# Linear attention beside a long convolution: denominators by groups of 512 tokens, new homes for the weights, and a new order of units

## The chip, the cores and the metric

The kernel runs on one core of a Trainium2 chip. The time is that of one execution on the device, in microseconds. A profiled execution gives a trace beside it: the span from its first to its last instruction, every instruction on every engine, and every DMA packet. The engines are PE (matrix products; its weight loads are listed as PEld), DVE, ACT and POOL (elementwise work), and SP, whose queue issues all DMAs of this kernel.

## What is computed

Two independent blocks, side by side in the output. Sequence length 2048, width 576, everything in bf16.

```python
# A: shift filter of 4 taps on k, times v, long causal convolution with ssm_k, times q
k_shift = sum(k_pad[:, t:t + S, :] * shift_k[:, 3 - t] for t in range(4))
kv = k_shift * v
y = irfft(rfft(kv, 2 * S) * rfft(ssm_k, 2 * S))[:S] + kv * ssm_D
a = q * y
# B: linear attention, 32 heads of 18
q, k, v = split(x @ wqkv)
phi = lambda t: where(t > 0, t + 1, exp(t)) + 1e-6
kv = einsum("bhsd,bhde", phi(k), v);  z = phi(k).sum(s)
o = (phi(q) @ kv) / ((phi(q) . z) + 1e-6)
b = o @ wo
return concatenate([a, b], -1)
```

## The kernel before, in words

The program is a list of units, `ORDER`. A unit is a name with arguments and, behind `@`, the PSUM banks (eight of 2 KB a partition) that its tiles take. The units are written out in that order, and each engine and the SP queue run their own instructions in the order of the list. An engine that must wait holds up everything behind it on that engine and nothing else. All waits follow from the data: an input must have been written, and a bank or a buffer must have been read to the end before it is written again.

**Block A.** The convolution is done with transforms as matrix products, in five chunks of channels (`ACH`: 128, 128, 64, 128, 128; chunk number is the first argument).

- `hl` loads ssm_k of a chunk and its D column. `hT` (L477) adds D to the first tap on ACT, turns the chunk with 16 PE transposes and evicts it.
- `h1`, `u1` (`s1`, L489): eight matmuls of 128 columns with the table G, for the filter h and the signal u = kv; the eviction goes to a tile C.
- `ht`, `ut` (`tr`, L503): SP issues a DMA transpose of half of C into a tile Ct. There are two Ct buffers, shared by h and u. The tag `c8` has two buffers as well, shared by C of h, C of u and V (L280), so a C can only be written when the transposes of an older one have landed.
- `h2`, `u2` (`s2`, L511): eight matmuls of 512 columns with 64x32 weights out of Ct into T or SU. `pX`, `pT` (`prod`, L526): products on DVE or POOL. `i1` and `j1` (L537, L551): 64 matmuls each of 64 columns, in four row groups; `j1` also evicts into V.
- `i2` (L562): 16 or 32 matmuls back to time, multiplied on DVE into q in place. `st` stores.
- `cv` (`conv`, L454): the four taps, in stages 0 to 3, eight operations of 128x2048 a chunk, each on DVE (`D`) or POOL (`P`). `Wj` (L376) spreads the taps over 128 partitions with matmuls whose weight is a row of ones. `kl`, `vl`, `ql` load k, v, q in two groups of channels; q takes the buffer of v.
- `io`, `ix`, `sin`, `iw`, `iv`, `wk`, `sw`, `W`, `FT`, `id` make the tables: index work on DVE and POOL, sines on ACT. `iv` (L186) has eight small operations on POOL (L192, L195) and one on DVE; `sw` (L217) takes the last sine and then loads the table of the exponential, so no exponential can come before it.

**Block B.** x is needed as it is (`xl`, L314, tile `x_sb`) and turned (`xT`, two buffers of 512 tokens). The turned x comes from `xd` (`x_D`, L342), two DMA transposes from DRAM and a memset on POOL for each group of 512 tokens. The functions `x_T` and `x_T2` (L325, L334) that turn it on PE stand in the file, but no unit calls them.

- `q` and `k` (L446, L430): five matmuls of 512 columns each; `kt` (L437) makes the last 64 columns of k for four token tiles. `phi` (L425) is an exponential on ACT and a min/max on DVE.
- `Gt` and `G` (L613, L627): x transposed times phi(k), five tiles, 16 matmuls each. `kv` (L635) multiplies by wv, `M` (L663) by wo, `z` (L653) makes the sums of phi(k).
- `den` (`b_den`, L671) makes the denominators of all 2048 tokens in one tile of 128x512, adds the epsilon on ACT and takes one reciprocal on DVE. `bc` (`b_bc`, L689) spreads 1/den over the channels of one of five chunks with four matmuls and multiplies phi(q) in place with two DVE operations of 1024 columns; it takes four banks.
- `o`, `ot` (L707, L714): output products of 128 tokens; `os` stores two token tiles.

Where buffers lie: wq and wk are one tile `wqk` (L306) with the tag `w12`. G and wv take that place afterwards (`wv_GT`, L587), so the first `Gt` must come after the last `q`. wo, M and the small kv tile take the place of phi(k) (`wo_M`, L600).

`fz` (L726) takes a bank; with `F` it also runs two matmuls whose result nobody reads. `wu.40` runs forty matmuls on zeros at the start.

Of the kernel before, what the change touches and what calls it, by code (L numbers as in the profile page):

```python
# [17 lines left out]
D = 576  # L18
# [12 lines left out]
ls wm io wu.0 Wj.0.A@0 Wj.2.A@2 wu.40@4 ix.0 sin.1 id ix.1 iw hl.0 hT.0.D@6 sin.0 lw.1 Wj.1.A@0 FT.1.D@2  # L31
h1.0.1.1.A@4 wk iv h1.0.0.1.D@6 xd.1 lw.0 h1.0.1.0.D@0 sw h1.0.0.0.D@2 W k.5@4 k.6@5 k.4@6 q.1.2@0 kt.1@1
FT.0.D@2 hl.1 hT.1.A@4 k.7@0 hc q.1.1@1 q.1.0@2 kl.0 cv.0.0.D h1.1.1.0.A@6 cv.0.1.DD one q.1.4@0 h1.1.0.0.A@4
q.1.3@1 xd.3 q.3.2@2 h1.1.1.1.A@6 k.13@3 q.3.0@4 q.3.3@0 cv.0.2.PD vl.0 h1.1.0.1.A@6 q.3.4@1 cv.0.3.DDD eps
ht.0.0 h2.0.0.1.A@2 h2.0.0.0.A@4 k.15@0 k.14@6 q.3.1@1 k.12@2 xd.0 kt.3@3 fz.9.N@4 k.3@4 ht.0.1 xl.0 q.0.4@0
cv.1.0.P cv.1.1.DD q.0.1@1 k.0@2 h2.0.1.0.A@6 h2.0.1.1.A@4 k.1@0 xl.1 q.0.2@3 u1.0.0.1.A@6 q.0.3@1 q.0.0@2
u1.0.1.0.A@4 cv.1.2.PD k.2@0 cv.1.3.DDD xd.2 ht.1.0 u1.0.1.1.A@6 u1.0.0.0.A@2 k.9@1 q.2.4@0 ht.1.1 h2.1.0.0.A@4
h2.1.0.1.A@6 k.8@2 q.2.1@3 u1.1.0.0.A@4 kt.0@1 kt.2@0 k.10@2 u1.1.1.1.A@6 xl.3 cv.2.0.P cv.2.1.PD cv.2.2.DP
q.2.0@1 h2.1.1.0.A@4 h2.1.1.1.D@2 u1.1.0.1.A@6 q.2.3@0 ut.0.0 u1.1.1.0.A@4 cv.2.3.PDD k.11@1 u2.0.0.1.A@6
u2.0.0.0.A@2 q.2.2@0 pX.0.0.D xl.2 Gt@4 hl.2 hT.2.A@6 fz.5.N@1 ut.0.1 pT.0.0.D u2.0.1.0.A@2 u2.0.1.1.A@0  # L40
pX.0.1.D pT.0.1.P ut.1.0 G.4@5 kl.1 u1.2.0.1.D@6 u1.2.1.1.A@2 u1.2.1.0.D@0 u2.1.0.1.A@4 u2.1.0.0.D@6 z@2
u1.2.0.0.A@0 ut.1.1 G.0@3 i1.0.1@40 ut.2.0 h1.2.1.0.A@6 h1.2.0.0.A@2 j1.0.1.AA@40 G.1@6 h1.2.0.1.A@2 cv.3.0.D
cv.3.1.DD cv.3.2.DD den@4 u2.1.1.0.A@0 u2.1.1.1.A@6 pX.1.1.D G.3@2 h1.2.1.1.A@0 bc.3@64 pT.1.1.D G.2@3 vl.1
cv.3.3.PDD i1.0.0@06 u2.2.0.0.A@4 j1.0.0.DA@06 lwv pX.1.0.P kv@2 hl.3 hT.3.A@4 ql.0 i2.0.0@6 i2.0.1@0
u2.2.0.1.A@2 ht.2.0 h2.2.0.0.A@4 cv.4.0.P h1.3.0.0.A@6 bc.0@20 lwo M.3@4 M.0@6 bc.4@24 i1.1.1@60 j1.1.1.DA@60
M.2@2 M.1@4 h2.2.0.1.A@0 h1.3.1.1.D@2 M.4@6 h1.3.1.0.A@4 h1.3.0.1.D@0 pT.1.0.P i1.1.0@26 j1.1.0.AA@26 bc.2@40
fz.4.F@2 bc.1@42 hl.4 hT.4.A@6 i2.1.1@0 i2.1.0@4 u1.3.1.1.A@2 ot.2.A@6 u1.3.0.1.A@0 ht.3.1 u1.3.1.0.D@2
u1.3.0.0.A@6 ot.3.D@4 h2.3.1.1.A@0 h2.3.1.0.D@2 ot.1.A@5 ht.3.0 h2.3.0.1.A@6 h2.3.0.0.D@0 h1.4.0.1.A@4
h1.4.1.1.A@2 h1.4.0.0.A@6 o.7.A@0 o.15.A@1 h1.4.1.0.A@4 ut.3.0 o.0.A@2 fz.7.F@0 u2.3.0.1.A@6 pX.2.0.P
u2.3.0.0.A@4 cv.4.1.PD cv.4.2.DD cv.4.3.DDD ut.3.1 pX.3.0.D pT.2.0.P i1.2.0@02 fz.0.N@6 j1.2.0.AA@02 o.9.D@6  # L50
u2.3.1.1.A@4 ht.4.0 u2.3.1.0.A@0 o.14.D@7 i2.2.1@2 i2.2.0@4 u1.4.1.1.A@6 u1.4.0.1.D@0 ht.4.1 u1.4.0.0.A@2
u1.4.1.0.A@4 ot.0.A@6 h2.4.0.1.D@0 os.7 h2.4.0.0.A@2 o.6.D@7 pT.3.0.P i1.3.0@40 ut.4.1 h2.4.1.1.A@2 h2.4.1.0.A@6
j1.3.0.AD@40 o.5.A@2 pX.3.1.P pT.3.1.D o.3.D@0 ut.4.0 u2.4.1.0.A@6 i1.3.1@42 u2.4.1.1.A@0 pX.4.1.D pT.4.1.D
o.12.A@6 j1.3.1.AA@42 u2.4.0.1.D@0 ql.1 o.4.A@6 os.3 os.2 o.1.A@2 i1.4.1@40 u2.4.0.0.A@6 pX.4.0.D pT.4.0.D os.0
j1.4.1.AA@40 o.8.A@2 st.0 i2.3.1@6 o.2.A@3 os.1 os.4 i1.4.0@40 j1.4.0.AD@40 o.13.A@2 os.6 i2.4.1@6 st.2 i2.4.0@4
i2.3.0@0 st.1 fz.1.F@2 o.11.A@3 fz.2.N@2 o.10.A@2 fz.8.N@0 os.5 fz.6.N@0 fz.3.N@0
# [178 lines left out]
def kernel(  # L235
# [70 lines left out]
    wqk = ab.tile([128, 5, 2 * D], BF, name="wqk", tag="w12")  # L306
# [123 lines left out]
    def b_k(r):  # L430
        ps = pt([128, 512])
        for t in range(5):
            nc.tensor.matmul(ps, lhsT=xT[r // 4][:, t, r % 4 * 128:(r % 4 + 1) * 128], rhs=wqk[:, t, D:D + 512],  # L433
                             start=(t == 0), stop=(t == 4))
        phi(ps, pk[:, r, 0:512], 128)

    def b_kt(g):  # L437

        ps = pt([128, 4, 64])
        for r in range(4):  # L440
            for t in range(5):
# [34 lines left out]

    def h_T(ci, eng='D'):  # L477
# [3 lines left out]
        nc.scalar.activation(out=h[0:dc, 0:1], in_=h[0:dc, 0:1], func=ACT.Identity, bias=s['D'][0:dc, :])  # L481
# [153 lines left out]
    def b_kv():  # L635
        wo_M()
# [7 lines left out]
        for c, (h0, hn) in enumerate(HCH):  # L644
            nc.vector.tensor_tensor(out=B['kvT'][0:hn, c, 0:hn], in0=ps[0:hn, c, 0:hn], in1=K.maskbd[0:hn, 0:hn],
# [25 lines left out]
    def b_den():  # L671
        B['rden'] = ab.tile([128, 512], BF, name="rden", tag="xT", bufs=2)
# [134 lines left out]
```

## Time and profile before

| what | value |
|---|---|
| three runs, median (lowest, highest) | 177.08 us (174.79 to 179.72) |
| the profiled execution, own time | 175.73 us |
| its span | 174.0 us |
| PE busy | 156.2 us, 90% |
| DVE, ACT, POOL busy | 136.3, 124.3, 82.6 us |
| DMA moved | 32.07 MB in 73,433 packets |
| chain that ended last | PE 65%, DMA 13%, ACT 8%, DVE 7% |

The chain is followed back from the last instruction to what released it at each step; shares are of the span. A wait is put down to the release that came last. Times below are from the start of the span. Busy time of PE runs from the first to the last moment of overlapping matmuls, so a full PE need not be at its peak rate.

### The profile page before, as it was taken

To read this page: it belongs to the slowest core of one execution; us is meant where nothing else is said; L and a number is where in the kernel's file an instruction comes from. 1 tells how busy PE (TensorE), PEld (TensorE's weight loads), DVE (VectorE), ACT (ScalarE), POOL (GpSimd) and SP (SyncE) were. 2 spreads that over 40 slices of the span, in tenths; PEclk is the share of its full clock that TensorE was granted. 3 is DMA by queue.
4 is the path that set the end of the run, shared out by engine and by line. 5 is a ranking of instruction groups with operands and counts; after the bars stand their busy time and mean duration, and the time that the engine had idled before them with its cause. 6 is when DMAs were issued, how large, how long until landed. Compare 5 with 4: busy or idle time off the path is not lost.

```text
span 174.0 us, 6216 instructions
## 1 busy us (share of the span) xinstructions
PE 156.2 (90%) x2763; PEld 99.5 (57%) x2763; DVE 136.3 (78%) x166; ACT 124.3 (71%) x160; POOL 82.6 (47%) x69
## 2 busy tenths in 40 slices
PE   4899998699999999999999997886899999679990
PEld 2885765345564757556544775656665574336650
DVE  7989788897979895899479969887489986265670
ACT  5698696685999997664762676964899998568511
POOL 7969906427360954082440599799400494000000
PEclk9999999999999999999999999999699999999999
DMA  4898989699997989699989930079086969978965
GB/s 122 186 232 252 293 181 273 145 176 316 140 215 195 228 175 146 160 218 167 300 277 267 249 121 0 4 134 114 0 128 121 164 152 132 229 202 266 304 199 188
DMA packets 73433, 32.07 MB, mean 184 GB/s; under 512 B 49283, under 2 KB 72829, under 8 KB 73406
## 3 DMA queue, kind: packets, MB, share of 16 engines
q1 hardware_dynamic: 73406, 31.68, 85.7%
q8 instruction: 21, 0.34, 0.8%
q14 instruction: 6, 0.05, 0.1%
HBM read 14.90 MB, written 4.72 MB: 113 GB/s over the span
## 4 chain that ended last, share of the span: by engine, by line
PE 65%; DMA 13%; ACT 8%; DVE 7%; issue 4%; ACTq 0%; DVEq 0%
PE banks L433 9%; DMA Cth<-Ch 9%; PE banks L450 9%; PE banks L631 8%; PE banks L710 7%; PE banks L498 6%; PE banks L548 5%; PE banks L522 5%; DMA Ctu<-Cu 4%; PE banks L485 3%; DVE rden L687 2%; PE banks L569 2%; PE banks L570 2%; ACT Cu L294 2%; PE banks L619 1%
## 5 line engine op out<-in xcount | busy, mean ns | idle before, releaser
L535 POOL TENSOR_TENSOR T<-SU,T 128x2048 bf16<-128x2048 bf16 x4 | 16.2, 4061 | 21.4 <-DVE X L533 21.4
L470 POOL TENSOR_TENSOR at<-k,Wj 128x2048 bf16<-128x2048 bf16 (+1 forms) x6 | 20.5, 3422 | 10.0 <-issue 5.5
L450 PE MATMUL banks<-xT,wqk 128*126 128x512 bf16 (+1 forms) x100 | 24.2, 380 | 0.7 <-POOL xT L348 0.7
L498 PEld LDWEIGHTS <-G 128*128 128x128 bf16 x320 | 18.2, 98 | 7.6 <-issue 4.3
L710 PE MATMUL banks<-wo_M,pqT 126*128 126x512 bf16 (+1 forms) x80 | 19.4, 380 | 0.5 <-ACT SU L294 0.3
L433 PE MATMUL banks<-wqk,xT 128*128 128x512 bf16 x80 | 19.4, 379 | 0.0
L294 ACT ACTIVATE SU<-banks 128x1024 bf16<-128x1024 f32 x16 | 15.8, 1033 | 3.4 <-PE banks L522 3.4
L631 PE MATMUL banks<-pk,x_sb 128*128 128x512 bf16 (+1 forms) x80 | 18.2, 379 | 0.0
L471 DVE TENSOR_TENSOR at<-at 128x2048 bf16<-128x2048 bf16 (+1 forms) x14 | 16.0, 1146 | 2.2 <-POOL at L470 1.8
L533 POOL TENSOR_TENSOR X<-SU,T 128x2048 bf16<-128x2048 bf16 x3 | 13.0, 4322 | 9.7 <-PE banks L548 8.4
L450 PEld LDWEIGHTS <-wqk 128*126 128x126 bf16 (+1 forms) x100 | 12.6, 131 | 8.4 <-DMA xT<-in_B_x_dram 0.6
L294 ACT ACTIVATE Cu<-banks 128x1024 bf16<-128x1024 f32 (+1 forms) x16 | 15.2, 972 | 3.1 <-DMA Cth<-Ch 2.5
L427 ACT ACTIVATE pqT<-banks,neg 126x512 bf16<-126x512 f32 (+1 forms) x20 | 13.9, 693 | 4.1 <-PE banks L450 4.1
L294 ACT ACTIVATE V<-banks 128x1024 bf16<-128x1024 f32 x14 | 14.3, 1060 | 3.1 <-PE banks L548 2.8
L294 ACT ACTIVATE T<-banks 128x1024 bf16<-128x1024 f32 x14 | 13.9, 1023 | 2.3 <-PE banks L522 2.3
L428 DVE SCALAR_TENSOR_TENSOR pqT<-pqT,banks 126x512 bf16<-126x512 bf16 (+1 forms) x20 | 13.4, 680 | 2.6 <-ACT pqT L427 2.6
L428 DVE SCALAR_TENSOR_TENSOR pk<-pk,banks 128x512 bf16<-128x512 bf16 (+1 forms) x20 | 12.2, 630 | 3.8 <-ACT pk L427 3.7
L427 ACT ACTIVATE pk<-banks,neg 128x512 bf16<-128x512 f32 (+1 forms) x20 | 12.7, 650 | 2.0 <-PE banks L433 2.0
L294 ACT ACTIVATE Ch<-banks 128x1024 bf16<-128x1024 f32 (+1 forms) x15 | 13.3, 913 | 0.4 <-PE banks L498 0.3
L294 ACT ACTIVATE ob<-banks 128x512 bf16<-128x512 f32 (+1 forms) x15 | 8.4, 570 | 7.1 <-PE banks L710 6.6
L468 POOL TENSOR_TENSOR at<-k,Wj 128x2048 bf16<-128x2048 bf16 (+1 forms) x3 | 10.2, 3413 | 6.2 <-DVE v L474 6.2
L631 PEld LDWEIGHTS <-x_sb 128*128 128x128 bf16 (+1 forms) x80 | 7.6, 100 | 9.2 <-issue 1.1
(129 smaller groups left out, 334.7 us busy)
## 6 DMA issues: line engine op xcount, KB each, us to landing
x_sb<-in_B_x_dram SPq DMA_DIRECT2D x4, 576.0 KB, 5.7
out_dram<-ob SPq DMA_DIRECT2D x8, 288.0 KB, 4.3
h_sb<-in_A_ssm_k_dram SPq DMA_DIRECT2D x4, 512.0 KB, 4.7
k<-in_A_k_dram SPq DMA_DIRECT2D x1, 1280.0 KB
v<-in_A_v_dram SPq DMA_DIRECT2D x1, 1280.0 KB
q<-in_A_q_dram SPq DMA_DIRECT2D x1, 1280.0 KB, 7.3
out_dram<-q SPq DMA_DIRECT2D x1, 1280.0 KB
wqk<-in_B_wqkv_dram SPq DMA_DIRECT2D x2, 576.0 KB, 4.7
```

The source lines that it names most:

```text
L294: nc.scalar.activation(out=out, in_=in_, func=ACT.Copy)
L427: nc.scalar.activation(out=out_ap, in_=ps_ap, func=ACT.Exp, bias=K.neg1[0:n, :])
L428: nc.vector.scalar_tensor_tensor(out=out_ap, in0=out_ap, scalar=1.0, in1=ps_ap, op0=ALU.min, op1=ALU.max)
L433: nc.tensor.matmul(ps, lhsT=xT[r // 4][:, t, r % 4 * 128:(r % 4 + 1) * 128], rhs=wqk[:, t, D:D + 512], start=(t == 0), stop=(t == 4))
L450: nc.tensor.matmul(ps[0:hn, :], lhsT=wqk[:, t, h0:h0 + hn], rhs=xT[g][:, t, :], start=(t == 0), stop=(t == 4))
L470: on[0].tensor_tensor(out=t_, in0=kk[:, 3 - stage:19 - stage], in1=wb(stage), op=ALU.mult)
L471: on[1].tensor_tensor(out=a_, in0=a_, in1=t_, op=ALU.add)
L498: nc.tensor.matmul(ps[:, bi, 0:dc].rearrange("p (z h y) -> p z h y", z=2, y=8), lhsT=K.G[ri][:, b, :], rhs=xf(b).rearrange("p (h z y) -> p ...
L533: on.tensor_tensor(out=s['X', hf][:], in0=s['SU', hf][:], in1=t[:, :, ::-1, :], op=ALU.mult)
L535: on.tensor_tensor(out=t[:], in0=s['SU', hf][:], in1=t[:], op=ALU.mult)
L631: nc.tensor.matmul(ps[0:fn, :], lhsT=x_sb[:, r, f0:f0 + fn], rhs=pk[:, r, 0:512], start=(r == 0), stop=(r == 15))
L710: nc.tensor.matmul(ps, lhsT=pqT[0:hn, c, r * 128:(r + 1) * 128], rhs=B['M'][0:hn, c, 0:512], start=(c == 0), stop=(c == 4))
```

## The change

1. **Denominators by groups of 512 tokens.** `b_den(g)` makes them for one group in a tile of 128x128, with its own bias and reciprocal; the epsilon part is a unit of its own, `ez`. `b_bc(g, c0)` multiplies one group: `bc.g.0` does the four chunks of 126 channels with 16 matmuls of 128 columns into four banks and four DVE operations of 512 columns; `bc.g.4` does the chunk of 72 with four matmuls and one DVE operation. `rden` no longer takes a buffer of the turned x.
2. **Weights.** wq and wk have tiles of their own. G takes the place of wk alone. wv joins wo, M and kv in the place of phi(k). wv and wo are loaded with two DMAs each, in place of five.
3. **x.** Groups 1 and 3 are turned by PE (`xT`, `xU`) out of `x_sb`; groups 0 and 2 stay with `xd`.
4. **`hd`.** The ACT operation that adds D leaves `hT` and is a unit of its own.
5. **The order** of all units, and which of ACT, DVE and POOL does an eviction or a product, are new. Two `fz` with matmuls stand in place of three.

```diff
-    wqk = ab.tile([128, 5, 2 * D], BF, name="wqk", tag="w12")
+    wq = ab.tile([128, 5, D], BF, name="wq")
+    wk = ab.tile([128, 5, D], BF, name="wk", tag="wk")
...
-            wg = B['wg'] = ab.tile([128, 2, 5, D], BF, name="wv_GT", tag="w12")
+            B['GT'] = ab.tile([128, 5, D], BF, name="GT", tag="wk")
...
+    def late_w():
+        if 'wo' not in B:
+            wm = big.tile([128, 16 * (D + 1)], BF, name="late_w", tag="pk")
+            n = 5 * D
+            for i, name in enumerate(('wo', 'M', 'wv')):
+                B[name] = wm[:, n * i:n * i + n].rearrange("p (c n) -> p c n", c=5)
+            B['kvT'] = wm[:, 3 * n:3 * n + D]
...
+    def b_den(g):
+        if 'rden' not in B:
+            B['rden'] = ab.tile([128, 4, 128], BF, name="rden")
+        ps = pt([128, 128])
+        for c, (h0, hn) in enumerate(HCH):
+            for j in range(4):
+                t0 = 512 * g + 128 * j
+                nc.tensor.matmul(ps[32 * j:32 * (j + 1), :], lhsT=B['zsel'][0:hn, c, :], rhs=pqT[0:hn, c, t0:t0 + 128],
                                  start=(c == 0), stop=(c == 4))
+        nc.scalar.activation(out=ps, in_=ps, func=ACT.Identity, bias=B['ez'][:])
+            nc.vector.reciprocal(out=B['rden'][:, g, :], in_=ps)
...
+    def b_bc(g, c0):
+        if c0 == 0:
+            ps = [pt([128, 4, 128]) for _ in range(4)]
+            for c in range(4):
+                hn = HCH[c][1]
+                for j in range(4):
+                    nc.tensor.matmul(ps[j][0:hn, c, :], lhsT=K.esel[32 * j:32 * j + 32, c, 0:hn],
+                                     rhs=B['rden'][32 * j:32 * j + 32, g, :], start=True, stop=True)
+            for j in range(4):
+                t0 = 512 * g + 128 * j
+                p = pqT[0:126, 0:4, t0:t0 + 128]
+                nc.vector.scalar_tensor_tensor(out=p, in0=p, scalar=EPS, in1=ps[j][0:126], op0=ALU.add, op1=ALU.mult)
...
```

The start of the new order, and the stretch around the two groups of q units that now stand behind G:

```
hl.0 io wu.0 eps id ix.0 ix.1 wu.40@0 hd.0 sin.1 hT.0.D@2 ls Wj.2.A@0 Wj.1.A@4 iw xl.1 xT.1.D@6 xU.1.A@0 xl.3
one wm Wj.0.A@2 h1.0.0.1.A@4 FT.1.D@0 iv xU.3.D@2 xT.3.D@6 sin.0 fz.0.N@3 fz.3.N@4 wk sw W lw.0 q.1.0@5 q.1.3@0
lw.1 k.6@1 k.7@2 k.15@3 k.4@4 kl.0 kt.1@0 cv.0.0.D cv.0.1.DD h1.0.1.1.A@6 cv.0.2.DD xl.2 q.3.2@1 h1.0.0.0.A@2
...
h1.1.0.1.A@4 xd.0 k.3@2 h1.1.1.0.A@0 k.2@3 k.1@4 xl.0 ht.0.0 h2.0.0.1.D@0 h2.0.0.0.A@6 k.0@2 u1.0.0.0.A@4
u1.0.0.1.A@6 cv.1.1.PD cv.1.2.DD kt.0@3 u1.0.1.0.A@0 q.0.1@2 u1.0.1.1.A@4 hT.2.D@6 xd.2 k.11@0 k.8@1 kt.2@3
k.10@2 ht.1.1 h2.1.1.0.A@4 cv.1.3.PDD h2.1.1.1.A@6 hl.3 hd.3 fz.1.N@0 k.9@1 Gt@0 ut.0.1 u2.0.1.1.A@2 ut.0.0
...
h1.2.0.1.A@2 h1.2.1.1.A@0 FT.0.D@4 h1.2.1.0.A@2 ez@6 den.1@0 den.3@1 u2.0.0.1.A@2 u2.0.0.0.D@4 pX.0.0.D G.0@6
ut.1.1 u2.1.1.0.A@2 u2.1.1.1.A@0 ut.1.0 h1.2.0.0.D@4 hT.3.D@6 u1.2.0.1.A@4 q.0.2@2 vl.1 u1.2.1.1.A@0 pT.0.0.P
...
j1.0.1.AA@06 ql.0 G.3@2 u2.1.0.1.A@4 ut.2.0 pX.1.0.D i1.0.0@06 pT.1.0.D h2.2.0.1.A@2 j1.0.0.AA@06 G.2@4
bc.1.0@0123 h1.3.1.0.A@6 q.2.4@4 lwv h1.3.0.0.A@0 i2.0.1@6 lwo u2.2.0.1.A@2 h2.2.0.0.A@4 i2.0.0@0 i1.1.0@26
pX.1.1.P j1.1.0.DA@26 h1.3.1.1.A@4 h1.3.0.1.A@0 ht.3.0 cv.4.0.D cv.4.1.DD kv@6 u2.2.0.0.A@2 pX.2.0.D pT.2.0.D
pT.1.1.P i1.1.1@40 j1.1.1.AA@40 q.0.3@2 q.2.2@3 M.4@6 M.1@4 fz.2.N@0 q.2.1@0 q.0.4@1 h2.3.0.0.A@6 i2.1.1@4 M.0@2
M.3@0 i2.1.0@6 i1.2.0@24 h2.3.0.1.A@0 j1.2.0.AD@24 hT.4.D@6 ht.3.1 M.2@0 u1.3.0.0.A@4 u1.3.0.1.D@2 u1.3.1.1.A@0
i2.2.0@6 u1.3.1.0.A@4 i2.2.1@2 h2.3.1.1.A@0 bc.1.4@4 den.0@2 den.2@3 h1.4.0.1.A@0 h2.3.1.0.A@4 h1.4.1.0.D@6
...
```

More of the change, by code (lines that the diff above doesn't have):

```diff
@@ L41 @@
[L41 to L45, printed above, removed]
@@ new lines, in b_bc @@
+    def b_bc(g, c0):
[10 more added lines that the diff above has]
+                nc.vector.scalar_tensor_tensor(out=p, in0=p, scalar=EPS, in1=ps[j][0:126], op0=ALU.add, op1=ALU.mult)
+        else:
+            hn = HCH[4][1]
+            ps = pt([128, 4, 512])
+            for j in range(4):
+                nc.tensor.matmul(ps[0:hn, j, 0:128], lhsT=K.esel[32 * j:32 * j + 32, 4, 0:hn],
+                                 rhs=B['rden'][32 * j:32 * j + 32, g, :], start=True, stop=True)
+            p = pqT[0:hn, 4, 512 * g:512 * g + 512].rearrange("p (j t) -> p j t", j=4)
+            nc.vector.scalar_tensor_tensor(out=p, in0=p, scalar=EPS, in1=ps[0:hn, :, 0:128], op0=ALU.add, op1=ALU.mult)
```

125 lines of the change are left out of this document (48 added, 77 removed).

## The prediction

> **What bounds the kernel now.** I read the page's head first, then busy time by stage, the chain of waits, the tile view of the turned copies, and the first microseconds of POOL.
>
> ```profile
> span 174.0 us, 6216 instructions
> PE 156.2 (90%) x2763; PEld 99.5 (57%) x2763; DVE 136.3 (78%) x166; ACT 124.3 (71%) x160; POOL 82.6 (47%) x69
> PE   4899998699999999999999997886899999679990
> PEclk9999999999999999999999999999699999999999
> ```
>
> PE is the bound: 17.8 us of the span are not PE, 8 of them the start and 4.4 the end (last matmul 169.6). What can be won are the holes between, near slices 24 to 26 and 33.
>
> ```profile
> 30.00:45.00 15.00, 13.64 (x114) 6.98 (x113) 12.77 (x17) 10.54 (x16) 6.98 (x4) 1.00 1.08 207
> 103.00:116.00 13.00, 9.97 (x337) 6.93 (x330) 11.24 (x10) 10.56 (x14) 11.79 (x4) 1.00 0.12 23
> 116.00:123.00 7.00, 4.93 (x93) 4.67 (x92) 4.92 (x5) 3.45 (x4) 7.00 (x2) 1.00 0.82 114
> 123.00:133.00 10.00, 10.00 (x131) 6.42 (x128) 8.19 (x8) 8.76 (x12) 0.67 (x1) 0.83 0.64 106
> 143.00:150.00 7.00, 5.42 (x228) 3.02 (x226) 3.86 (x5) 4.44 (x6) 2.55 (x1) 1.00 1.16 145
> ```
>
> Columns: stretch, length, busy PE, PEld, DVE, ACT, POOL, granted clock, DMA share, GB/s. Idle PE: 1.36, 3.03, 2.07, 0 and 1.58 us. In the fourth row PE is full, but the clock was 0.83: half speed for 3.4 us, 1.7 us lost.
>
> ```profile
> 114.04 1.23 DVE pqT L700
> ...
> 115.29 6.03 DMA Cth<-Ch
> ...
> 121.42 1.03 ACT Cu L294
> ...
> 142.51 6.52 DMA Ctu<-Cu
> ```
>
> ```profile
> DMA to landing us min/median/max: 5.0/5.7/6.5
> 3.88 5.70 POOL L192 TENSOR_SCALAR sm<-sm 128x32 int32<-128x32 f32 x6
> ```
>
> The holes are waits for the 1/den products (L700, 1.23 us on four banks), for a slot of C that a turning DMA still reads (6.03), and for a turned copy (6.52; 5.0 to 6.5 in general). The last line matters at the start.
>
> **The change part by part.** Sums are against the profiled execution: span 174.0, own time 175.73, which is 0.8% under the median 177.08 of the three runs.
>
> *Denominators by group.* Before: reciprocal 3.36 + ten products of 1.21 = 15.5 us of DVE. After: four reciprocals of 128 columns (a quarter of 3.36 each, or up to 0.97 with 0.17 fixed, as the smallest DVE rows have: 3.4 to 3.9) and 20 products of 512 columns at 0.68 (the L428 row): 17.4, so +2. ACT: four biases at 0.3 (288 ns is its 128x1 row) for one of 0.66: +0.5. PE: 20 matmuls of 512 took 1.19 in four column strips; 80 of 128 take the same if the strips still overlap, as L548 does (64 in 0.61), and 4.5 if they run at 56 ns each; I take 1.2, nearest L548. The product matmuls likewise: five fours of 0.43 before (L696); 80 of 128 columns after, 1.5 at L548's overlap, 4.5 at 56 ns each; I take 1.5, 0.7 less. DVE's and ACT's share hides beside G (3.46 us a unit, one ACT eviction) and the q units; without that cover +2.5. What goes is the four-bank wait: most of the 3.03.
>
> *Own tiles.* GT no longer waits for the last q, so five q units (1.08 each, L450) stand behind the last G and fill 95 to 111. Their exp and min/max (0.69, 0.68) land on ACT and DVE there. wv and wo (four DMAs in place of ten, which held SP for 7.5 us) now issue only after the last G has read pk; between that G and kv stand 7.1 us of units in the order, against 4.7 for a 576 KB weight load and 7.9 for the slowest load row: 0 to 0.8; I take 0.
>
> *x by PE.* 40 transposes at 56 ns (16 in 0.89, L578): +2.2 on PE; evictions 1.2+1.2+0.35 DVE, 0.6 ACT; four DMA transposes leave SP (5.2+1.25+8.4+1.25 us of issue), two x loads move to the front of SP, ahead of both weights. h, x, x and wq are 2.35 MB; before moved 2.3 MB in its first 13 us, so wq is there for a q unit at 14.8. One fill pair goes (-0.43). PE work: +2.2-0.43-0.7 = +1.1.
>
> *Order, start.* DVE does ident, L142, L144, L149 (5.7 us) to 7.5, then hT's copy (8.85), and only then the memset of ones that Wj needs: PE waits until 9.1. Then 5.65 us of units in the new order: first q at 14.8, against 12.66 before for the first k, with 0.9 us more done: +1.2. Six L192 on POOL now stand behind the memset of the turned x (12.8); DVE's index op, the last sine and the exp table follow them. Undisturbed they take 0.36 each as L195 does, first exp at 18.2 (14.38 before), and PE, with five banks in hand, does not stop. At their mean here, 0.95, PE stops 3.3 us. I take the first, since the memsets and PSUM reads beside them look like L195's surroundings: +1.2, ends 0 and 4.5.
>
> *Order, 36 to 56.* xd.0, xl.0, ht.0.0, xd.2 and ht.1.1 stand in SP's queue within 20 us, in a stretch whose DMA share was 1.08 before. By the queue they land within 1 us of need. I take +1.0 (0 to 2.5); the 1.36 of 33 to 34.5 goes, its copy now having 10 us.
>
> *Order, ut.1.1.* Its slot comes free with u2.0.0.0; only G.0 (3.46) stands before its reader. 5.7-3.5 = 2.2 of wait (1.5 to 3.0).
>
> *Order, from the last G.* I laid the units in order on PE, ACT, DVE and POOL with their rows, each starting when its engine, bank and input were there. Cu of chunk 3 finds its slot free 5 us early, so 2.07 and the half clock behind it go. But 18 short waits for banks remain (0.1 to 0.55, mostly behind ACT, which has 33 us of work for 31 of PE), 3.3 in sum (2 to 5): den.0 for i2.2.1's product 0.25, bc.2.4 for DVE's eviction of h1.4.1.0 0.55, h2.3.1.0 behind ACT 0.45, i2.4.0 for V 0.4 are the kind. Four copies have 4.8 to 6.2 us between issue and use: 1.6 at a landing of 5.7, 4 at 6.5. Five conv operations of 4.06 go to POOL, 106 to 126, needed at 130: hidden. All eight of chunk 3 go to DVE, 9.8 us from 81.6; G.1 and G.3 cover them, and pX.1.0 behind them is not read before i1.1.0. h's D add leaves hT and goes ahead on ACT, 0.29 each, hidden as before.
>
> *The half clock.* At 120.0 to 123.4 PE was busy 1.4 of 3.4 us and the next 3.4 ran at 0.5. The new 2.2 us wait may do this again: 0 or 1.7; I take 0.8.
>
> **Sum.** Gone: 3.03+2.07+1.7+1.58+1.36 = 9.7. Come: work 1.1, start 1.2, queue 1.0, ut.1.1 2.2, banks 3.3, copies 1.6, clock 0.8 = 11.2. Net +1.5: span 175.5, own time 177.2; on the median 177.08 x 177.2/175.73 = 178.6.
>
> On the clock, the Trainium skill (TensorE: Matmul & The Clock Gate, Part 1) says that activity is judged in free-running windows of 3413 ns; the 3.4 us at half clock agree. It also says (Part 4) that transposes do not count as busy; no row here shows that. By it the sum would gain the cold start below.
>
> **Rivals.**
> Faster: the holes go and few come. Gone 9.7; come work 1.1, start 1.2, ut.1.1 2.2, copies 0.8, and no bank waits, because ACT works ahead while PE does q units: -4.4, own time 171.3, 172.6 on the median. For it: DMA is at 0.12 and 0.82 in 103 to 123, room for the moved work. Against: ACT is at 10.6 of 13 already there and gets more.
> Slow POOL at the start: L192 as slow as in its row. +3.3 more: 180.5, 181.9 on the median. It is the one that decides for slower, from about 0.8 us per L192 up. For it: the row. Against: L195, 0.36, same shape.
> Cold start: PE's forty warming matmuls end at 5.4 instead of 7.5 (they took 4.14, 103 ns each, twice the later 56), then come 16 transposes and a hole to 9.1. If no full window falls into them, 9.1 to 16 runs at half clock: two windows, +3.4: 180.6, 182.0. Against: before had a hole of 0.5 us at 7.5 and stayed warm.
> No change from the parts: the waits were only shifted; that is the forecast itself.
>
> **How the numbers follow.** Forecast 0.50 (175 to 181.5 alone), faster rival 0.22, slow POOL 0.15, cold start 0.13. Range: at the low end the faster rival at its own number, which leaves out about half of its chance, 0.1; at the high end a slow rival (182) with 2 more from the upper bounds of copies and queue, which leaves out 0.1 more: 172.5 to 184. About 2% is what this measurement tells from no change: 173.5 and 180.6. Faster 0.20 (the rival, less its part above 173.5, plus the forecast's low edge), same 0.47, slower 0.33 (both slow rivals and the forecast's upper edge).
>
> **What would show it.** Right: first exp near 18; PE idle about 2 us before u2.1.1.0 near 75; no idle of 2 us between 103 and 123; ACT fuller than PE from 95 to 125; 80 den matmuls in about 1.2 us. Wrong: first exp after 20; matmuls of 128 at 107 ns after 9; a kv that waits for wv; holes of over 2 us between 36 and 56; or a tail without holes.

## The result and the profile after

The changed kernel took 200.79 us at the median of four runs (199.1 to 202.32), the kernel before 176.32 beside it (174.79 to 179.72): 1.133 times as long, 95% interval 1.116 to 1.151. The forecast was 178.6, the range 172.5 to 184.0; the time lies 17 us above the range. Where a run below has a median and no ratio, its executions, or those of the kernel before beside them, spread too widely for an interval.

The head of the page after, with PE and its granted clock in 40 slices:

```profile
span 197.4 us, 6533 instructions
...
PE 166.0 (84%) x2908; PEld 107.4 (54%) x2921; DVE 160.2 (81%) x185; ACT 127.0 (64%) x166; POOL 79.1 (40%) x66
...
PE   7499998996999960999988999639999949869991
...
PEclk9966999999999996699999999975999988979997
```

PE is 9.8 us longer busy and 13.6 us longer idle (197.4 - 166.0 = 31.4, against 17.8). DVE is 23.9 us longer busy, though the forecast gave it 2 us of new work for the denominators and about 3 for the turned x. Before, one slice stood at 0.6 of the clock. Now ten stand below 0.9, five of them at 0.5 or 0.6: at the start, behind the holes of 6.8, 4.2, 2.7 and 2.2 us, and behind the last matmul. Three stretches (columns as in the table before: length, busy PE, PEld, DVE, ACT, POOL, granted clock, DMA share, GB/s):

```profile
70.00:80.00 10.00, 3.20 (x34) 1.53 (x32) 9.19 (x7) 3.06 (x5) 6.14 (x3) 0.80 0.11 23
120.00:130.00 10.00, 6.67 (x86) 4.17 (x73) 9.97 (x8) 6.62 (x10) 9.73 (x3) 1.00 0.64 97
8.00:20.00 12.00, 10.76 (x81) 8.01 (x83) 8.47 (x21) 9.23 (x12) 6.14 (x16) 0.72 1.12 313
```

In the first, PE waits for 6.8 us while DVE is full with seven instructions. Which seven the timeline says, behind one row from before (start, duration, engine, line, operation; in brackets the idle time before it and what ended that):

```profile
66.42 0.69 DVE L474 TENSOR_TENSOR at<-at 128x1024 bf16<-128x1024 bf16 x1
67.15 4.43 DVE L473 TENSOR_TENSOR at<-k,Wj 128x1024 bf16<-128x1024 bf16 x1
71.61 4.43 DVE L474 TENSOR_TENSOR at<-at 128x1024 bf16<-128x1024 bf16 x1
75.96 0.67 DVE L431 SCALAR_TENSOR_TENSOR pqT<-pqT,banks 126x512 bf16<-126x512 bf16 x1
76.56 0.68 DVE L473 TENSOR_TENSOR at<-k,Wj 128x1024 bf16<-128x1024 bf16 x1
77.27 0.69 DVE L474 TENSOR_TENSOR at<-at 128x1024 bf16<-128x1024 bf16 x1
78.00 0.69 DVE L477 TENSOR_TENSOR v<-at,v 128x1024 bf16<-128x1024 bf16 x1
78.61 0.68 DVE L431 SCALAR_TENSOR_TENSOR pqT<-pqT,banks 126x512 bf16<-126x512 bf16 x1
...
66.55 4.48 POOL L541 TENSOR_TENSOR X<-SU,T 128x2048 bf16<-128x2048 bf16 x1 [5.85 <-ACT SU L295]
71.11 4.38 POOL L543 TENSOR_TENSOR T<-SU,T 128x2048 bf16<-128x2048 bf16 x1
...
79.34 0.63 PE L530 MATMUL banks<-Cth,W 64*32 64x512 bf16 x8 [6.80 <-DVE pqT L431]
```

The same sum of 128x1024 took 0.69 us at 66.42 and 4.43 at 71.61. The two long ones begin behind the start of a POOL product and end 0.55 us behind its end. Behind them stand, with three short taps between, the min/max of two q units (L431 at 75.96 and 78.61), whose banks PE needs next; it goes on when the second is done. The same pairing stands at 43.76 (4.44), 120.88 (4.38), 125.30 (4.96) and 155.08 (4.79). DVE operations that read PSUM keep their time beside POOL: the 1/den products (L713) at 109.48 to 111.28, beside a POOL product, take 0.68 each as elsewhere. The row of DVE's T products carries the clash too:

```profile
L543 DVE TENSOR_TENSOR T<-SU,T 128x2048 bf16<-128x2048 bf16 x6 | 14.6, 2440 | 0.1
...
L471 DVE TENSOR_TENSOR at<-k,Wj 128x2048 bf16<-128x2048 bf16 x4 | 8.6, 2160 | 0.0
```

Before, the like row had a mean of 1218 ns, and one row of conv products stood out:

```profile
L535 DVE TENSOR_TENSOR T<-SU,T 128x2048 bf16<-128x2048 bf16 x5 | 6.1, 1218 | 0.1
...
L468 DVE TENSOR_TENSOR at<-k,Wj 128x2048 bf16<-128x2048 bf16 x2 | 3.5, 1725 | 0.0
```

**Theory (lock):** a DVE operation that takes its inputs from SBUF stands still while a POOL product runs; the holes that follow also bring half clock. **Rivals:** the new order, with more DVE work and new bank waits, is the cause and POOL is incidental; POOL and DVE share bandwidth; the start, where the clock was 0.72, is the cause.

### The profile page after: what moved, and what is told of

Same layout as the page of the kernel before. It is cut to its first block, busy times and chain, and to the rows that moved or that the text cites. A ratio compares the mean times of both kernels' runs of the same rounds, so it can differ in the third digit from the quotient of the medians.

```text
span 197.4 us, 6533 instructions
## 1 busy us (share of the span) xinstructions
PE 166.0 (84%) x2908; PEld 107.4 (54%) x2921; DVE 160.2 (81%) x185; ACT 127.0 (64%) x166; POOL 79.1 (40%) x66
## 4 chain that ended last, share of the span: by engine, by line
PE 55%; DVE 30%; issue 6%; ACT 4%; DMA 2%; SPq 0%; DVEq 0%; ACTq 0%
PE banks L731 10%; PE banks L637 7%; DVE at L474 6%; PE banks L436 6%; DVE at L473 6%; PE banks L556 5%; PE banks L453 5%; PE banks L506 4%; PE banks L530 4%; DVE at L471 4%; DVE pqT L431 3%; DVE T L543 3%; DMA Dcol<-in_A_ssm_D_dram 2%; PE banks L493 2%; DVE X L541 2%
## 5 line engine op out<-in xcount | busy, mean ns | idle before, releaser
L541 POOL TENSOR_TENSOR X<-SU,T 128x2048 bf16<-128x2048 bf16 x4 | 17.3, 4346 | 25.4 <-ACT SU L295 14.1
L453 PE MATMUL banks<-xT,wq 128*126 128x512 bf16 (+1 forms) x100 | 26.1, 400 | 0.6 <-DVE pqT L431 0.6
L473 POOL TENSOR_TENSOR at<-k,Wj 128x2048 bf16<-128x2048 bf16 x4 | 17.1, 4276 | 17.5 <-DVE at L474 12.3
L731 PE MATMUL banks<-late_w,pqT 126*128 126x512 bf16 (+1 forms) x80 | 21.2, 414 | 0.1
L430 ACT ACTIVATE pqT<-banks,neg 126x512 bf16<-126x512 f32 (+1 forms) x20 | 13.6, 691 | 10.4 <-PE banks L453 10.2
L436 PE MATMUL banks<-wk,xT 128*128 128x512 bf16 x73 | 18.2, 379 | 0.6 <-DVE pk L431 0.2
L637 PE MATMUL banks<-pk,x_sb 128*128 128x512 bf16 (+1 forms) x76 | 17.8, 379 | 0.2
L543 POOL TENSOR_TENSOR T<-SU,T 128x2048 bf16<-128x2048 bf16 x3 | 12.5, 4174 | 12.4 <-DVE X L541 12.2
L453 PEld LDWEIGHTS <-wq 128*126 128x126 bf16 (+1 forms) x100 | 12.7, 139 | 7.7 <-issue 2.3
L473 DVE TENSOR_TENSOR at<-k,Wj 128x2048 bf16<-128x2048 bf16 (+1 forms) x11 | 16.1, 1463 | 0.2
L431 DVE SCALAR_TENSOR_TENSOR pqT<-pqT,banks 126x512 bf16<-126x512 bf16 (+1 forms) x20 | 13.0, 679 | 3.4 <-ACT pqT L430 3.4
L530 PE MATMUL banks<-Cth,W 64*32 64x512 bf16 x144 | 7.7, 413 | 9.0 <-DVE pqT L431 8.4
L543 DVE TENSOR_TENSOR T<-SU,T 128x2048 bf16<-128x2048 bf16 x6 | 14.6, 2440 | 0.1
L431 DVE SCALAR_TENSOR_TENSOR pk<-pk,banks 128x512 bf16<-128x512 bf16 (+1 forms) x20 | 12.2, 629 | 3.0 <-ACT pk L430 2.9
```

The source lines that it names most:

```text
L430: nc.scalar.activation(out=out_ap, in_=ps_ap, func=ACT.Exp, bias=K.neg1[0:n, :])
L431: nc.vector.scalar_tensor_tensor(out=out_ap, in0=out_ap, scalar=1.0, in1=ps_ap, op0=ALU.min, op1=ALU.max)
L453: nc.tensor.matmul(ps[0:hn, :], lhsT=wq[:, t, h0:h0 + hn], rhs=xT[g][:, t, :], start=(t == 0), stop=(t == 4))
L473: on[0].tensor_tensor(out=t_, in0=kk[:, 3 - stage:19 - stage], in1=wb(stage), op=ALU.mult)
L541: on.tensor_tensor(out=s['X', hf][:], in0=s['SU', hf][:], in1=t[:, :, ::-1, :], op=ALU.mult)
L543: on.tensor_tensor(out=t[:], in0=s['SU', hf][:], in1=t[:], op=ALU.mult)
```

## The experiments

### The pair by itself

```python
for v, nv, g, ng in ((v_tt, 5, None, 0), (None, 0, g_tt, 2), (v_tt, 5, g_tt, 2), (v_tt_ps, 7, g_tt, 2), ...
```

> Measures the disputed pair by itself; nothing of the reference is computed (the output is zeros). Stages, each begun by two ACT copies: five DVE products with both inputs in SBUF (128x2048 bf16) alone; two POOL products alone; the five beside the two; then, always beside two POOL products, DVE products with one input in PSUM, DVE copies out of SBUF, DVE copies out of PSUM, DVE scalar_tensor_tensor with both inputs in SBUF and with one in PSUM; five DVE products beside three POOL memsets; eight DVE products of 512 columns beside one POOL product; four DVE products beside eight POOL products of 256 columns. Lock theory: DVE alone 1.22 us each, POOL alone 4.06; together a DVE product with both inputs in SBUF that meets a POOL product ends only with it (4 to 5 us), while the ones with a PSUM input keep the time that they have alone; POOL's own goes from 4.06 to 4.4 to 4.9. For copies out of SBUF and for memsets no row has shown anything: left open. Rival, shared bandwidth: every DVE operation that touches SBUF is slowed by about the same factor for as long as POOL runs, the ones with a PSUM input too. Rival, no clash: all pairs as alone, and the long DVE rows of the changed kernel came from something else.

The timeline, DVE first and POOL behind; `d` and `g` lie in SBUF, `ps` in PSUM:

```profile
16.85 6.25 DVE L35 TENSOR_TENSOR do<-d,d 128x2048 bf16<-128x2048 bf16 x5
28.73 19.59 DVE L35 TENSOR_TENSOR do<-d,d 128x2048 bf16<-128x2048 bf16 x5 [5.64 <-ACT d L31]
50.35 8.77 DVE L38 TENSOR_TENSOR do<-ps,d 128x1024 bf16<-128x1024 f32 x7 [2.03 <-ACT d L31]
...
63.35 4.42 DVE L41 COPY do<-d 128x2048 bf16<-128x2048 bf16 x1
...
119.64 6.27 DVE L35 TENSOR_TENSOR do<-d,d 128x2048 bf16<-128x2048 bf16 x5 [2.04 <-ACT d L31]
...
26.98 9.03 POOL L53 TENSOR_TENSOR go<-g,g 128x2048 bf16<-128x2048 bf16 x2 [26.54 <-ACT g L32]
38.03 9.21 POOL L53 TENSOR_TENSOR go<-g,g 128x2048 bf16<-128x2048 bf16 x2 [2.02 <-ACT g L32]
52.20 8.19 POOL L53 TENSOR_TENSOR go<-g,g 128x2048 bf16<-128x2048 bf16 x2 [4.96 <-ACT g L32]
...
118.94 5.53 POOL L56 MEMSET go<- 128x2048 bf16 x3
```

Five DVE products take 6.25 us alone and 19.59 beside four POOL products (the stage meant for POOL alone ran beside them). With one input in PSUM seven take 8.77 us, 1.25 each, and POOL keeps 4.1; beside memsets five take 6.27. That is the lock: not a factor on everything, but a wait for the end of POOL's instruction. One thing is wider than the theory: a copy with a single SBUF input waits too (0.69 us alone, 4.42 at 63.35). A scalar_tensor_tensor from SBUF took 6.03 (2.29 alone), from PSUM 1.22.

### POOL's work given to DVE, all or two of it

```diff
-pX.0.1.P pT.0.1.P
+pX.0.1.D pT.0.1.D
```

The first run does this for all 14 operations, the second for these two.

> The changed kernel with the 14 conv operations and products that it puts on POOL given to DVE, each at its place; nothing else is changed. DVE gets 14 x 1.22 = 17.1 us of work more than if each kept its time alone. Lock theory: the 22.6 us that DVE stood still go, so DVE busy falls from 160.2 to about 155, the PE holes at 47 (2.0), 72.5 to 79.3 (6.8), 126.7 to 132.1 (4.6) and 157.4 (2.7) go with most of the half clock behind them (6.6): own time from 199.1 to 175 to 184. Rival, the order (bank and buffer waits, more DVE and ACT work for denominators and products are what holds PE): 17 us more on an engine that is 81% busy, 200 to 212. Rival, clock at the start alone: 197 to 201.

> The changed kernel with two POOL operations alone, the two products of half 1 of chunk 0 near 66 to 75 us, given to DVE. Lock theory: the two DVE conv operations of 4.43 take 0.63 to 0.7 again (they are 128x1024), DVE gets 2 x 1.22 in return, so 5 us of the hole of 6.8 at 72.5 to 79.3 and the half clock at 75.9 to 82.7 (3.2 us lost) go: own time 199.1 to 190 to 193, and the later clashes stay. Rival, the order: DVE has 2.4 us more in a stretch where it is 92% busy, 199 to 203.

The first took 198.39 us, 1.122 times before (1.112 to 1.131): above the lock theory's 184, a little below the order's 200, and inside the 197 to 201 named for the clock at the start. DVE fell to 155.8 us busy, no row is long, and yet nothing is won. Two groups of PE in its page (busy and mean; idle time before, and what ended it):

```profile
L556 PE MATMUL banks<-W,T 32*128 32x64 bf16 x576 | 11.5, 196 | 7.2 <-DVE T L543 6.5
...
L506 PE MATMUL banks<-v,G 128*128 128x128 bf16 (+1 forms) x160 | 11.5, 233 | 6.9 <-DVE v L477 6.9
```

The 17 us now stand in DVE's queue ahead of what PE waits for: pT.1.1, read at once, came behind the taps of chunk 4. So this run cannot tell the theories apart; it takes one wait away and puts in another. The second run, 191.29 to 199.0 with a median of 197.19, decides nothing by its time; in its trace the two operations take 0.69 us, and a hole of 2.19 stands in place of 6.80.

### The start

```diff
-hl.0 io wu.0 eps id ix.0 ix.1 wu.40@0 hd.0 sin.1 hT.0.D@2 ls Wj.2.A@0 ...
+hl.0 io wu.0 eps id ls ix.0 ix.1 wu.54@0 hd.0 sin.1 hT.0.D@2  Wj.2.A@0 ...
```

> The changed kernel with its start alone changed: the memset of ones and the load of the taps go ahead of the index operations, and 54 warming matmuls run in place of 40. Lock theory with the clock as its second part: the hole of 1.4 us before 9.18 goes and the first 7 us of work run at full clock, 3.4 us less lost and up to 1 us of the hole: own time 199.1 to 195 to 197, and all long DVE rows stay. Rival, the start is bound by DVE's and ACT's index work and by loads, not by PE: within 0.5 us of 199.1, with holes in the first 20 us in place of the half clock. If the clock were all of it: 180 or less.

197.56 us (194.18 to 198.35), 3.2 below the changed kernel's median, and in the profiled execution 4.9 below. The first q matmul starts at 13.32 in place of 16.68, at full clock. The start is one loss of 3 to 5 us, not the main one.

### The same order, POOL busy without reading

```diff
-        on = nc.gpsimd if eng == 'P' else nc.vector
+        class Fill:
...
+                nc.gpsimd.tensor_tensor(out=out[:, :, :, 0:8], in0=in0[:, :, :, 0:8], in1=in1[:, :, :, 0:8], op=op)
+                for _ in range(2):
+                    nc.gpsimd.memset(out, 1.0)
...
+        on = Fill if eng == 'P' else nc.vector
```

> The changed kernel, same order, same engines, same 14 operations on POOL, but each is made of a product of a few columns (which waits for the same inputs) and two memsets of the whole output, 3.7 us beside 4.06: these 14 products and sums are left out, so the output holds wrong numbers in their places. In the measurement of pairs POOL's memsets did not hold up DVE (five products in 6.27 us beside them, 6.25 alone), its products did. Lock theory: no DVE row of a product or sum over 1.3 us is left, DVE busy falls by about 20 from 160.2, the PE holes near 48, 72.5 to 79 and 127 to 131 go, and their half clock: own time 199.1 to 178 to 187, the start's 3 to 5 us stay lost. Rival, the new order's DVE queue is too full or wrongly sorted with or without POOL (so read from the run without POOL work, 198.4): 193 to 200.

> The changed kernel with POOL's 14 operations as memsets (the products and sums on POOL are left out, as in the earlier run of that kind) and the mended start: what the change would take with neither the lock nor the cold start. Both theories of two separate losses: 176.95 less the 3 to 5 of the start, 172 to 174. Rival, what the start gains is lost again at the next wait when nothing else is in the way: 176 to 177.

The second run has the mended start as well. The first took 176.95 us (175.98 to 177.25), 23.8 below the changed kernel, with the same order, the same queues and POOL nearly as long busy (74.2 us against 79.1):

```profile
span 175.4 us, 6577 instructions
...
PE 160.4 (91%) x2921; PEld 104.0 (59%) x2921; DVE 139.5 (80%) x185; ACT 126.7 (72%) x166; POOL 74.2 (42%) x94
```

DVE is 20.7 us less busy. The span is 22.0 shorter: 16.4 of PE's idle time and 5.6 of its busy time, with 10.2 us at half clock up to the last matmul in place of 27.3. The holes of 1.59 (48), 6.80, 4.23 (130) and 2.71 us (160) are gone; 1.59 and 1.45 at the start stay, and so does one at the tail (2.22 us at 174 in the changed kernel, here 2.78 at 151). This refutes the rival of the order: the order works when POOL does not read. It was better than the 178 to 187 expected.

The hole at the tail is a loss of its own. Here and in the second run it reads:

```profile
151.08 0.62 PE L537 MATMUL banks<-Ctu,W 64*32 64x512 bf16 x6 [2.78 <-issue]
...
148.29 0.41 PE L722 MATMUL banks<-rden,esel 32*126 32x128 bf16 x12 [2.13 <-issue]
```

The units differ, but the place in PE's stream is the same: in all twelve runs with the new order a hole of 1.2 to 2.8 us stands ahead of matmul 2514 or 2526 of the record (some records are missing), and nothing on record ends it ("issue"). Each time it ends 2.4 to 2.7 us after the start of a 16 KB packet on queue q8, which the page lists as instructions. That PE waits there for its own instructions is likely, but no run varied it.

With the mended start on top it is 174.26 us, 0.990 times before (0.978 to 1.002), its span 172.1. The two losses nearly add: 22.0 and 4.9 of span each by itself, 25.3 together.

### The lock put into the kernel before

```diff
-pT.2.0.P i1.2.0@02
+pT.2.0.P dx i1.2.0@02
...
+for _ in range(3):
+    nc.gpsimd.tensor_tensor(out=t, in0=t, in1=t, op=ALU.mult)
```

The second run has seven memsets of `t` in the loop.

> The kernel before with three more products on POOL (128x2048 bf16 on free columns of a tile, 12.2 us), which nothing waits for, queued behind pT.2.0 near 124 us, where POOL is idle for 13.8 us and DVE does seven operations with both inputs in SBUF from 128.7 to 137.4. All is computed. Lock theory: two or three of the seven last 4 to 5 us, the chain ends 6 to 9 later, the time of before rises by 3 to 9 us. Rival, POOL's work beside DVE is harmless: no change (within 1 us).

> The same place with seven memsets (128x2048 bf16, 1.80 us each, 12.6 in all) in place of the three products. Lock theory: DVE's seven keep 1.22 each and the time is that of before within 1 us. Rival, any busy POOL in that stretch slows the kernel: as the run with the products.

With products 186.24 us, 1.059 times before (1.050 to 1.068), 10 us more where 3 to 9 were expected, though nothing waits for them:

```profile
132.12 4.51 DVE L470 TENSOR_TENSOR at<-k,Wj 128x2048 bf16<-128x2048 bf16 x1
136.66 4.50 DVE L471 TENSOR_TENSOR at<-at 128x2048 bf16<-128x2048 bf16 x1
...
127.40 12.68 POOL L752 TENSOR_TENSOR wo_M<-wo_M 128x2048 bf16<-128x2048 bf16 x3
```

A product and a sum stand still, PE then has a hole of 5.73 us, up to 146.7, and half clock goes with it. With memsets POOL is as long busy at the same place:

```profile
125.73 12.99 POOL L752 MEMSET wo_M<- 128x2048 bf16 x7
```

Here the seven DVE operations keep 1.22 each; the time is 178.77 (175.3 to 179.38) beside 175.82 (174.81 to 179.65), not to be told from it.

### POOL's work cut into pieces

```diff
-        on = [nc.gpsimd if e == 'P' else nc.vector for e in eng]
+        class Pieces:
...
+                for i in range(0, 16, 2):
+                    r = slice(i, i + 2)
+                    nc.gpsimd.tensor_tensor(out=out[:, r], in0=in0[:, r], in1=in1[:, r], op=op)
...
+        on = [Pieces if e == 'P' else nc.vector for e in eng]
```

The second and third run have four pieces and the mended start.

> The changed kernel, same order and engines, with each of the 14 POOL operations cut into eight of a quarter of a thousand columns (256). All is computed. In the measurement of pairs a DVE product lasted 1.57 in place of 1.23 beside POOL products of 256 columns (0.67 each alone), and 4.95 beside those of 2048. Lock theory: what a DVE operation loses is the rest of one POOL instruction, so no DVE row of a product or sum over 2.2 is left, DVE busy falls from 160 to 143 to 152, while POOL needs 5.9 us for what took 4.06 (chunk 4's five: 30, ready at about 151 where u1.4 reads near 150): own time 178 to 190. Rival, shared bandwidth or the order: POOL's work is the same and lasts longer, 197 to 205.

> The changed kernel with its POOL operations cut into four of 512 columns (estimate 1.1 to 1.2 us each, 4.7 in all) and the mended start (taps first, 54 warming matmuls). Lock theory: a DVE operation loses 1.1 at most, about 12 less than now in sum, and the start's 3 to 5 us: 178 to 188. Rival: 193 to 198, as with the mended start alone (197.6).

> The kernel with POOL's operations in four pieces and the mended start (180.3), with the last taps of chunk 2 moved on DVE behind z and so behind the min/max of q.2.0, which PE waits for at 70 us (hole of 3.0, half clock behind it). All is computed. Lock theory, by which the three long taps (1.5 in place of 0.69 each) fill that hole: the hole goes or shrinks to under 1.5 and its half clock goes, 175 to 179. Rival: the wait moves to the load of k behind chunk 2, 180 or more.

All is computed, in the order of the change. Eight pieces: 193.38 us, 1.096 times before (1.090 to 1.103), 7 less than the changed kernel and 3 above the range expected. Four pieces and the mended start: 180.28 (176.72 to 185.17), 20.5 less. With four, the two operations of chunk 2 take 1.53 us in place of 4.43. With eight, one operation did not get its turn between the pieces (L557 is L543 of the changed kernel, L550 the pieces):

```profile
147.17 6.04 DVE L557 TENSOR_TENSOR T<-SU,T 128x2048 bf16<-128x2048 bf16 x1 [2.95 <-POOL X L550]
...
142.10 10.02 POOL L550 TENSOR_TENSOR X<-SU,T 128x256 bf16<-128x256 bf16 x16
```

DVE waited through the last eight pieces, of which the first had just begun, and PE had a hole of 6.99 behind it; elsewhere in the same run the two engines took turns (1.04 us for a sum of 0.69). What decides this stays open. The third run moved chunk 2's last three taps behind the min/max that PE waited for: 182.17 (179.11 to 184.33), no gain. The hole of 3.03 us up to 70.3 became one of 2.96 up to 73.6, now for the table F, which stands behind the same taps. The rival had it right, with another wait than it named.

### Sorting and placing

```diff
-pX.1.1.P ... cv.4.0.D cv.4.1.DD kv@6 u2.2.0.0.A@2 pX.2.0.D pT.2.0.D pT.1.1.P
+pX.1.1.D pT.1.1.D ... kv@6 u2.2.0.0.A@2 pX.2.0.D pT.2.0.D
```

In the sorted kernel the taps of chunk 4 go behind M.1 and later. The placed kernel also has chunk 2's products ahead of them, but leaves nine operations on POOL. All three runs have the mended start.

> The changed kernel with POOL's 14 operations on DVE, the mended start (taps first, 54 warming matmuls), and DVE's queue sorted by need: the two products of chunk 0 half 1 behind the eviction that they held up, pT of chunk 1 half 1 ahead of the taps of chunk 4, and these taps where DVE was half idle (120 to 130 us in the run without POOL work) and so before their reader near 150. If the run without POOL work was lost only because the same 17 us stood ahead of urgent work in DVE's queue: its holes of 2.2 at 77, 6.5 at 118 and 6.6 at 153 go with about 5 us of half clock, and the start's 4 us: 174 to 182. Rival, the total of DVE work is the bound of this order (155.8 us busy): holes of the same sum elsewhere, 190 to 197.

> The changed kernel with the clashes taken away by place: five of the 14 POOL operations (cv.1.1, the two of chunk 0 half 1, the two of chunk 3 that met pT.3.0) on DVE, chunk 2's products ahead of chunk 4's taps on DVE so that POOL's five taps begin after them, the mended start, whole POOL operations. Lock theory: DVE has 6 us more work, loses 22 less: at most two DVE rows over 2 us, own time 174 to 183. Rival (the sum of two-input work is too much for this order, as in the sorted run with none on POOL, 188.7): 187 to 192.

> The placed kernel of this call with its nine POOL operations cut into four. Lock theory: what is left of clashes costs up to 1.1 us each in place of 3.5, POOL's own work gets 0.6 longer each: within 2 us of the placed one if that has no clashes, 2 to 6 faster if it has.

Sorted, none on POOL: 188.66 us (187.72 to 191.44), between the 174 to 182 of the one theory and the 190 to 197 of the other; placed: 183.82, 1.042 times before (1.035 to 1.049), just above its 174 to 183; placed in pieces: 183.27, 1.041 (1.035 to 1.047). Fewer clashes help, but what takes their place costs: 155.2 us of DVE work in the sorted run leave holes of 1.9, 1.9 and 3.4 between 108 and 128, each behind DVE or an ACT that waits for it. No version that computes everything beats the kernel before; the 174.26 above, which leaves POOL's results out, is not below it beyond its interval either.

### Denominators by groups alone

```diff
-den@4
+ez@5 den.2@4 den.1@5 den.3@4 den.0@5
```

The five old products became eight, in the same banks and places.

> The kernel before with one part of the change alone: denominators, reciprocal and products by groups of 512 tokens, the four groups at the places where the old units stood, in the banks that these had. Forecast's price: DVE +2, ACT +0.5, PE -0.7 for the products, and two waits of several banks less or more: within 2 us of before (ratio 0.99 to 1.012). Rival, the grouping is a main part of the loss (20 products with 16 small weights each, four reciprocals on the chain): ratio above 1.03.

184.9 us (183.93 to 188.75) beside 178.16 (172.04 to 180.2), by the medians 1.038: dearer than the forecast's price and, as far as medians go, on the rival's side of 1.03. PE's waits for the products and reciprocals come to 7.2 us, 4.8 of it in four waits of 0.80 to 1.93 between 110 and 125; before, its waits behind the products were 0.97 in all. This prices the part in the old places only. In the new order without the lock, PE waits for these products nowhere over 1.3 us.

### The clock by itself

```python
for cols in ((384,), (896,), (1408,), (1920,), (2048, 640), ...):
    for rep in range(4):
        for n in cols:
            V.tensor_copy(out=do[:, 0:n], in_=ps[:, 0:n])
        burst(60 + rep)
```

> Measures the clock by itself; nothing of the reference is computed (the output is zeros). Bursts of 60 to 63 matmuls of 512 columns (about 13 us) with holes between them that last as long as one to three DVE copies out of the bank: about 0.6, 1.2, 1.7, 2.2, 3, 4 and 5.5 us, four of each. From the traces of both kernels (half clock for 3.4 us behind holes of 2.05, 2.2, 2.7 us, for 6.8 behind 4.2 and 6.8; none behind holes of 1.3 to 1.6 in mid-run): no half clock up to about 1.7, then 3.4 us of it behind a part of the holes from 2 us on, according to where the hole lies, and behind all from 4 us on. Rival: it needs 3.4 us without a matmul; then nothing behind 2.2 and 3.

Four bursts of 61 matmuls (in brackets the hole before), and the granted clock (the figure behind POOL's) behind a hole that ended at 206.34:

```profile
100.51 13.32 PE L28 MATMUL ps<-r,w 128*128 128x512 bf16 x61 [1.18 <-DVE do L41]
160.04 13.33 PE L28 MATMUL ps<-r,w 128*128 128x512 bf16 x61 [1.72 <-DVE do L41]
223.39 15.01 PE L28 MATMUL ps<-r,w 128*128 128x512 bf16 x61 [2.25 <-DVE do L41]
296.08 15.01 PE L28 MATMUL ps<-r,w 128*128 128x512 bf16 x61 [3.24 <-DVE do L41]
```

```profile
206.00:207.00 1.00, 0.66 (x4) 0.30 (x4) 0.29 (x1) 0.00 (x0) 1.00 0.00 0
207.00:208.00 1.00, 1.00 (x5) 0.42 (x4) 0.00 (x0) 0.00 (x0) 0.82 0.00 0
208.00:209.00 1.00, 1.00 (x4) 0.40 (x3) 0.00 (x0) 0.00 (x0) 0.50 0.00 0
```

None of the twelve holes up to 1.72 us cost clock; all four of 2.25 cost 1.7 us, those of 3.24 cost 1.6 to 2.9, and the eight longer ones 1.3 to 2.8, a part of the half clock lying in the hole. The rival (3.4 us needed) is out, and up to 1.72 us the theory holds.

That every hole of 2.25 cost, and not a part, does not refute "according to where the hole lies". In every trace of this case in which it changes, the clock does so only at whole multiples of 3.413 us from one change to the next, as if it were judged step by step (the prediction's windows). The half clocks behind these four holes begin at 207.64, 224.71, 241.77 and 258.84, five such steps apart each, so that all four holes lay in their step alike, with 2.1 to 2.25 us inside it. In the sorted kernel the end of a step, at 163.20, cut a hole of 2.22 us (162.38 to 164.60) into 0.82 and 1.40, and no half clock followed. Counted over 17 traces between start and last matmul, in steps at full clock: with 1.88 us or more of idle PE in the step, half clock followed in 45 of 45; with less than 1.6, in 2 of 761; between them, in 6 of 11.

## Why the prediction was wrong

**The step that failed** is "From the last G", and with it all of "I laid the units in order on PE, ACT, DVE and POOL with their rows": each operation was given the time of its row, as if POOL's and DVE's times were independent. "Five conv operations of 4.06 go to POOL, 106 to 126, needed at 130: hidden" is the plainest place. They ran from 120 on; what they held up were DVE's two products of chunk 2 (4.38 and 4.96 where 1.22 each was counted), and PE stood for 4.23 us behind these. Cover was asked of POOL's reader alone, not of the engine beside it. This is 22.0 us of span; without it the time was 176.95.

The sign stood in the profile of before, on both sides. POOL's L192 had a mean of 0.95 us, in the prediction's own fence: three of the six, of 0.91, 1.18 and 2.36, end 0.16 us behind a DVE operation on SBUF each (these end at 4.63, 5.89 and 8.32), the other three took 0.29, and the neighbour L195 0.36. The prediction made that a rival for the start, even with the remark that PSUM reads beside it are harmless, and did not ask what DVE loses by the same pairing. And DVE's L468 had a mean of 1725 ns for two, one of 1.23 and one of 2.23 (at 77.69), which lay over the end of a POOL product; its other such operations had 1.22. The order before had one such long one, the order after has six of 4.38 us and more.

The Trainium skill states the rule (SBUF — State Buffer, section Who interferes with whom): a DVE instruction with two SBUF inputs and a GpSimd instruction that reads SBUF exclude each other for the whole instruction, and one that only writes does not. The traces agree: 4.95 against 1.23 us beside products, 1.23 beside memsets.

**Cold start** came with the length and the price that this rival had: half clock from 11.1 to 17.9, two windows, priced at 3.4; the two memset runs differ by 3.3 of span. Its path was another. The record has full clock from 4.25 to 11.08, so the warming matmuls did bring it, and it was lost again: the step before 11.08 holds PE's hole of 1.45 us and for the rest transposes and matmuls of one row. The rule on transposes that the prediction quotes would fit this; no run separates the two. It was no alternative to the forecast, though, but added to the rest. **Slow POOL** did not come: the six took 2.11 us from first to last, 0.35 each, and the first exponential started at 18.57 (forecast 18.2).

**The other terms**, read in the run with neither lock nor cold start, span 172.1 against the forecast's 175.5 (its start is the mended one):
- The start, +1.2: by the terms PE is idle for 4.0 us up to 15 (2.8 before, and 1.2). The memset run with the start as forecast has 4.2, which is right, but with half clock behind it, which had no term; the mended start has 1.3. The 8 us of idle time that the prediction saw at the start of before are these 2.8; no term rests on it.
- ut.1.1, 2.2 of wait near 75: not there. PE is idle 0.11 us between 70 and 80.
- The queue between 36 and 56, +1.0: not there, 0.21 idle in 20 us. These three are 5.7 us less; 2.3 of it came back in half clock, PE's work and waits elsewhere.
- From the last G, waits for banks 3.3 and copies 1.6: PE idles 5.4 us between 95 and 150, where before it was 6.8. Its terms leave 6.75 - 3.03 - 2.07 - 1.58 + 3.3 + 1.6 = 5.0. The sum is right, its make-up is in part luck: waits for banks behind ACT took 1.9, copies 0.9, and 2.1 is the hole at 148.29, for which there was no term. The 3.03 counted as gone were read as waits for the 1/den products; in the trace of before these end 0.97 of them, ACT's evictions 2.06.
- Denominators: the four reciprocals 3.5 us in sum, the products 0.68 each, as forecast; 40 matmuls of den in 0.75, so 1.5 for 1.2.
- PE's work +1.1: 157.6 busy against 156.2, +1.4, about 1 of it for the 14 more warming matmuls of the mended start (54 took 5.08 us, 40 before 4.14).
- The half clock, 0.8: the mechanism held, its size hung on the holes. By the clock's record 27.3 us of after ran at half clock up to the last matmul, against 3.4 before.

## What to carry to other kernels

Before an elementwise operation goes to POOL, ask what DVE does at that moment: where it works out of SBUF, the two take turns by whole instructions, and the offload gives back one DVE operation of 1.22 us for a wait of 3.2 to 3.7. Put POOL's long reads where DVE evicts PSUM, or cut them short. A row whose mean is more than its fellows' is worth a look at the timeline for what runs beside it, on both engines.

## What the runs showed of the hardware

- A DVE copy with one SBUF input and a scalar_tensor_tensor from SBUF wait for POOL's product as a product does (0.69 us to 4.42, 2.29 to 6.03). POOL waits as well: its 4.05 went to 4.91 behind a DVE product and to 5.97 behind the scalar_tensor_tensor.
- Among dense matmuls half clock came behind every hole of 2.25 us and more and behind none of 1.72 or less, but what counted was the idle time inside one step of 3.413 us: about half of a step (1.88 us, 45 of 45), in one hole or in several. It begins at the step's end, so behind the holes of 2.25 the matmuls first ran 0.7 to 1.3 us at full clock, then 3.4 at half. The Trainium skill (TensorE: Matmul & The Clock Gate, Part 1) puts the gap that matters at over some 3.4 us; the measurement decides, it is shorter here.
- The record of the clock can say 1.00 where matmuls run slow: in the run with two operations moved, 16 transposes near 18 us took 1.91 us at a recorded 1.00, as in the changed kernel at 0.50; warm they take 1.07. That run's first record is a change to full clock at 20.61; ahead of the first record 1.00 says nothing.
